# One of three shifted readings of a VectorE attention unit is made on GpSimd, with a new list of units

## The chip, the cores and the metric

The kernel runs on one core of a Trainium2 chip. The core has five engines that run their own instruction streams in order and meet only at semaphores: TensorE (PE in the profile) multiplies matrices into PSUM, ScalarE (ACT) evaluates functions such as the exponential, VectorE (DVE) and GpSimd (POOL) do elementwise arithmetic, SyncE (SP) issues DMAs. The metric is the device time of one execution in microseconds (us). Before the change it is 1565.71 us, the median of three runs (1563.85 to 1565.89).

## The reference

Two layers are computed on x of 2048 positions by 512 features. Each layer is an attention block and a gated mixer, both added to x:

```python
# attention: 32 query heads of width 16, one shared key and value head
scores = einsum('bhqd,bkd->bhqk', q, k) * 16 ** -0.5
p = softmax(scores, axis=-1)
x = x + einsum('bhqk,bkd->bhqd', p, v) @ wo          # on layernorm(x)
# mixer: width 896, mixed over the 2048 positions
z = gelu(layernorm(x) @ w_in); z1, z2 = z[:, :896], layernorm(z[:, 896:])
x = x + (z1 * (w_sp @ z2 + b_sp)) @ w_out
```

The attention has 32 x 2048 x 2048 exponentials in each layer, and they are what most of the time goes to.

## The kernel before

**Units.** The attention of a layer is cut into 32 groups (`GROUPS`; the index is gi). A group is four heads with all their 512 columns of queries, so that a tile of scores is 128 keys by 512 query columns. A group has 16 key tiles (kt), and the four heads of one key tile are a unit: four score tiles, their exponentials, and the product of these with the values (PV), which is summed over the key tiles in one PSUM bank, `PVB`. The softmax's sum comes out of the same product, from a column of ones beside the values.

**Two ways to make a unit.** `push_unit` gives a unit to ScalarE. Its blocks go through PSUM in slots of three or two blocks (`push_slot`); one ACTIVATE of L950 turns a slot into exponentials in `P_ring`. Slots alternate between a wide one (three banks) and a two-bank one; in the groups whose bit is set in `NARROW` the wide one has two blocks too. The PV of such a unit is four products at L969.

`push_unit_dve` gives a unit to VectorE. Scores come scaled so that adding a constant and writing the sum as a 16-bit integer gives the bit pattern of a bfloat16 that lies near the exponential. Four instructions of L1003 do this, one for each head, from PSUM into a tile of `big` of 128 x 2048. One such reading of the bits has a periodic error, so `NPH` = 3 readings are used: the first, and two that have 43 and 86 added to every 16-bit word (`PH_A`). These two are the instructions of L1012, each from 128 x 2048 int16 to 128 x 2048 int16 in SBUF. Each reading is multiplied with values that carry its own weight (`V_ph`), in four products at L1018, so a VectorE unit has three sets of PV products where a ScalarE unit has one. The tiles of `big` are a ring of 5, 6 or 8 (`phr`), and a tile can be written again when the PV products that read it are done.

`ON_DVE[layer][gi]` lists the key tiles of each group that VectorE makes: 245 of the 1024 units.

**Order.** The order on every engine is written out ahead of time by a planner, `_Graph.schedule`. Each operation has an engine, a planned duration, the operations it depends on and a priority (a lower number goes first). The planner runs the engines forward in planned time and lets each take the ready operation with the lowest number. `emit` then writes one fixed instruction stream for each engine, with a semaphore wait for each dependence. On VectorE the L1003 instructions have priority `P_R` = 0.3 and the L1012 ones `P_A` = 4.0. So where the next unit's scores are ready, its L1003 instructions stand ahead of the L1012 ones of this unit. Scores for VectorE units use PSUM banks that are free at that time, above all banks 5 and 7 (`side`).

**What else the engines do.** During a layer's attention, work of the same and the next layer is spread between the units: layer norms (L817, L818, L823, with `rstd` on GpSimd at L805 and L807), the projections (PE, L713), the first parts of the mixer (`b_front`, `mix_stage`; VectorE L1213, L1239, L1350), and what ends a group. At the end of a group VectorE copies the PV bank into `oT` (L1091), a DMA turns it into `ot`, and GpSimd raises the sums to the power -1 (L1048) and multiplies by them (L1061). In the last part of each layer GpSimd also takes some of the products of L1419. Where PE would have nothing to do the planner adds products with zeros or ones (L740, L751) that keep its clock up.

Of the kernel before, what the change touches and what calls it, by code (L numbers as in the profile page):

```python
# [6 lines left out]
FP32 = mybir.dt.float32  # L7
BF16 = mybir.dt.bfloat16
I16 = mybir.dt.int16
ACTF = mybir.ActivationFunctionType  # L10
ALU = mybir.AluOpType
AX = mybir.AxisListType
# [16 lines left out]
PH_A = (0, 43, 86)  # L29
# [15 lines left out]
HOLDS = 1.0  # L45

ON_DVE = ((
          (6,10,14), (6,10,14), (6,10,14), (6,10,14), (2,6,9,12,14), (2,3,12,13,14), (2,4,6,11,13),
          (3,4,6,7,9,14), (2,3,6,11), (5,7,8,13), (2,7,8,10,14), (4,5,6,12), (2,9,12,13,14), (2,9,10,13,14),
          (3,5,8), (2,6,7,14), (5,7,9,12,14), (6,8,9,10), (3,9,12,13,14), (2,7,9,13), (2,5,10,13), (2,8,11,12),  # L50
          (7,9,12,13,14), (2,7,9,12), (5,6,8,13), (4,10), (3,7,14), (2,7,10,14), (3,8,9,14), (2,9,14),
          (6,10,14), (2,9,12)
), (
          (6,10,14), (6,10,14), (10,14), (14,), (6,10,14), (6,10,14), (6,10,14), (2,10,14), (2,7,8,11),
          (6,8,10,12,14), (3,6,9,12), (3,5,8,9), (2,7,11,12,14), (2,3,9,11), (4,6,9,12), (2,4,11,12),
          (5,6,9,13), (4,6,8,9,14), (2,5,10,12), (2,7,8,10,14), (2,4,7,14), (4,8,10,11), (3,4,6,10,14),
          (6,9,12,14), (2,6,14), (2,3,12,13,14), (6,), (2,4,6,12,14), (6,8,13), (2,9,12), (3,10,11,13),
          (3,8,12)
))


# [18 lines left out]
BEFORE = ({0: 0}, {0: 0})  # L80
PRE = 6
CHAIN_ACT = 1
NARROW = (4194528, 10506244)
KEEP = 6
POOL_ON = 1
POOL_XN = 0
POOL_Z2 = 0
KEY_PR = {0: 1.2, 2: 1.7, 4: 2.2, 6: 2.4, 8: 2.7, 10: 2.9, 12: 3.2}
# [11 lines left out]
P_A = 4.0  # L100
# [64 lines left out]
class _Graph:  # L165
# [29 lines left out]
    def op(self, eng, fn, dur, r=(), w=(), prio=5, lat=0.0, chan=None, mode=0):  # L195
        task = next((x for x in (*w, *r) if isinstance(x, _Task)), None)
        o = _Op(eng, fn, dur, lat, prio, len(self.ops), chan, task, mode)
        o.chain = self.chain
        if task is not None:
            task.ops.append(o)  # L200
        if chan is not None:
            n = self.chans.setdefault(chan, 0) + 1
            self.chans[chan] = n
            o.chan_val = 16 * n

        def dep(p, kind):
            if p is o:
                return
            if p.eng == eng and p.chan is None:
                k = 0 if eng == "pe" else 1  # L210
            else:
                k = 1
            o.deps[p] = max(o.deps.get(p, 0), k)

        for key in r:
            p = self.last_w.get(key)
            if p is not None:
                dep(p, "raw")
        for key in w:
            p = self.last_w.get(key)  # L220
            if p is not None:
                dep(p, "waw")
            for q in self.readers.get(key, ()):
                dep(q, "war")
        for key in r:
            self.readers.setdefault(key, []).append(o)
        for key in w:
            self.last_w[key] = o
            self.readers[key] = []
        self.ops.append(o)  # L230
        return o
# [336 lines left out]
def bass_interleave_layers__grouped_kv_mqa__mixer_gmlp__prompt_kernel(  # L568
# [15 lines left out]
    P = 128  # L584
    NT = S // P
    QC = 512
    NQC = S // QC
    CT = QC // P
    G = _Graph(nc, (5, 7), ((0, 1, 2), (3, 4), (0, 1)))
    op = G.op  # L590
# [5 lines left out]
    def bank32(b, n=1):  # L596
        return ps32[:, 512 * b:512 * (b + n)]
# [13 lines left out]
    idle = G.sb([P, 1], FP32, "idle")  # L611
    mhalf = G.sb([P, 1], FP32, "mhalf")
    mone = G.sb([P, CT], FP32, "mone")
    X = G.sb([P, NT, D], BF16, "X")

    kT_rep = G.sb([P, 2, S], BF16, "kT_rep")
# [36 lines left out]
    NRING = 6  # L653
    big = G.sb([P, 8, 2048], BF16, "big")
    ph16 = big[:].bitcast(I16)
    wspL = big[:, 4:6, :].rearrange("p a (t q) -> p a t q", q=QC)
    gbuf32 = big[:].bitcast(FP32).rearrange("p a (b q) -> p (a b) q", q=QC)
    oT = G.sb([P, 2, QC], BF16, "oT")
# [16 lines left out]
    def BIG(r):  # L675
        return [("big", r, 0), ("big", r, 1)]
# [12 lines left out]
    def dve(fn, us, r, w, prio=5):  # L689
        return op("dve", fn, max(us - DVE_LAT, 0.06), r=r, w=w, prio=prio, lat=DVE_LAT)  # L690
# [36 lines left out]
                                         pattern=[[-1, P]], channel_multiplier=1), 0.3, r=["ident"], w=["ident"])  # L727
    op("pool", lambda e: e.memset(mhalf[:], -0.5), 0.1, w=["mhalf"])
    op("pool", lambda e: e.memset(mone[:], -1.0), 0.1, w=["mone"])
    op("pool", lambda e: e.memset(zeros[:], 0.0), 0.2, w=["zeros"])  # L730
    G.warm_after = op("pool", lambda e: e.memset(ones[:], 1.0), 0.2, w=["ones"])
    G.pvb = PVB
# [79 lines left out]
    def ln_tiles(t0, n, xT, keys, per_tile, prio=5):  # L812
# [7 lines left out]
        for t in ts:  # L820
            i = t % CT
            on_pool = POOL_XN and not G.chain and (now["layer"] or t0 >= CT or xT is xo)
            op("pool" if on_pool else "dve", lambda e, i=i, t=t: e.tensor_scalar(  # L823
# [52 lines left out]
    def q_slot(si, pr=3):  # L876
# [13 lines left out]
        if G.chain and si < CHAIN_ACT:  # L890
            op("act", lambda e: e.activation(qT[:, si % NQ, :], bank32(tk.bank), ACTF.Copy, scale=Q_SCALE), 0.48, r=[tk],
               w=[("q", si % NQ)], prio=1, lat=ACT_LAT)
# [10 lines left out]
    def next_slot():  # L903

        if main["i"] % 2:
            return 1, 3, 2
        return (2, 0, 2) if NARROW[now["layer"]] >> now["gi"] & 1 else (0, 0, 3)

# [19 lines left out]
    def push_slot(n):  # L928
# [20 lines left out]
        def act_e(e):  # L949
            return e.activation(P_ring[:, s0:s0 + n, :], bank32(b0, n).rearrange("p (k q) -> p k q", k=n), ACTF.Exp,  # L950
                                scale=E_SCALE)
# [35 lines left out]
    def push_unit_dve(u):  # L987

        hg, kt, first, last = u[:4]
        assert not first and not last  # L990
        tiles = [phr["base"] + (phr["n"] + a) % phr["ring"] for a in range(NPH)]
        phr["n"] += NPH
        first_op = None
        heads = {"left": [0, 1, 2, 3], "of": {}, "hold": HOLD_DVE[now["group"] // 8]}
        for j in range(4):
            tk = _Task()
            box = []
            o = op("pe", lambda e, box=box, tk=tk: scores(e, bank32(tk.bank), u, heads["of"][box[0]]), TILED, r=[("K", hg[1], kt), ("q", hg[0])],
                   w=[tk], prio=P_S, lat=PE_LAT, mode=1)
            o.work = WORK_OP / 4  # L1000
            o.heads = heads
            box.append(o)
            o = dve(lambda e, box=box, tk=tk: e.tensor_scalar(  # L1003
                ph16[:, tiles[0], heads["of"][box[0]] * QC:(heads["of"][box[0]] + 1) * QC], bank32(tk.bank), PH_BIAS, 0.0, op0=ALU.add, op1=ALU.max),
                0.69, [tk], BIG(tiles[0]) if j == 0 else [("phj", tiles[0], j)], P_R)
            if j == 0:
                first_op = o
            else:
                o.deps.update({q: k for q, k in first_op.deps.items() if q.task is not first_op.task})
        base = BIG(tiles[0]) + [("phj", tiles[0], j) for j in range(1, 4)]  # L1010
        for a in range(1, NPH):
            dve(lambda e, a=a: e.tensor_scalar(ph16[:, tiles[a], :], ph16[:, tiles[0], :], float(PH_A[a]), None,  # L1012
                                               op0=ALU.add), 0.69, base, BIG(tiles[a]), P_A)
        for a in range(NPH):
            def pe_pv(e, a=a):
                ins = None
                for j in range(4):
                    ins = e.matmul(bank32(PVB)[32 * j:32 * j + 32, :], V_ph[:, a, kt, :],  # L1018
                                   big[:, tiles[a], j * QC:(j + 1) * QC], tile_position=(0, 32 * j), start=False,
                                   stop=False)  # L1020
                return ins
            pv_op(pe_pv, (base if a == 0 else BIG(tiles[a])) + [("V", kt)], False, False, TILED)
# [3 lines left out]
    def finish_group(gi):  # L1026
# [15 lines left out]
        def src():  # L1042
            if not isinstance(tk, _Task):
                return ot[:, par, :, :].rearrange("p b (j r) -> p b j r", j=4)
            return bank16(tk.bank)[:, 0:CT * P].rearrange("p (b j r) -> p b j r", b=CT, j=4)
        on_pool = POOL_ON and not G.chain
        if on_pool:
# [142 lines left out]
    def b_front(t0, n, g0):  # L1190
# [8 lines left out]
        for t in ts:  # L1199
            i = t % CT  # L1200
            for h in range(2):
# [6 lines left out]
                if fine:  # L1208
                    op("act", lambda e, t=t, h=h, tk=tk: e.activation(
                        z2n[:, t, h * 448:(h + 1) * 448], bank32(tk.bank)[:, 0:448], ACTF.Gelu_apprx_tanh), 0.55,  # L1210
                        r=[tk], w=[("z2", t, h)], prio=1)
# [6 lines left out]
        for f0 in range(0, NF1, nf):  # L1218
# [16 lines left out]
            if fine:  # L1235
                op("act", lambda e, dst=dst, src=src: e.activation(dst(), src(), ACTF.Gelu_apprx_tanh), 0.60,
                   r=[tk], w=zk, prio=2)
# [6 lines left out]
        if not fine:  # L1244
            z2k = [x for t in ts for x in Z2(t)]

            def act_g(e):
                v = z2n[:, g0:t1, :]
                return e.activation(v, v, ACTF.Gelu_apprx_tanh)  # L1249
            if g0 >= Z2_LATE[now["layer"]]:  # L1250
# [11 lines left out]
    def gelu_rest():  # L1262
# [6 lines left out]
        for g0, t1 in parts:  # L1269
            k = [x for t in range(g0, t1) for x in Z2(t)]  # L1270
            v = z2n[:, g0:t1, :]
            op("act", lambda e, v=v: e.activation(v, v, ACTF.Gelu_apprx_tanh), us + 0.2 + 0.75 * (t1 - g0), r=k + ["lastexp"],
               w=k, prio=0.2)
# [204 lines left out]
    now = {"tail": False}  # L1478
# [60 lines left out]
```

## Time and profile before

| | |
|---|---|
| median of three runs | 1565.71 us (1563.85 to 1565.89) |
| the profiled execution, its own time | 1566.62 us |
| its span in the profile | 1564.7 us |
| granted TensorE clock | 0.997 |
| PE / ACT / DVE / POOL busy | 1492.9 / 1484.2 / 1379.3 / 330.3 us |
| L1003, VectorE, from PSUM | 980 of 684 ns |
| L1012, VectorE, SBUF to SBUF | 490 of 687 ns |
| L950, ScalarE, 128 x 1536 and 128 x 1024 | 538 and 751 |

The span runs from the first instruction to the last; the execution's own time has 1.9 us around it. Busy times are unions of the records of an engine, and records of successive instructions can overlap a little, as one starts while the one before it drains. A line of the profile such as "L1012 DVE TENSOR_SCALAR big<-big 128x2048 int16<-128x2048 int16 x490" names the source line, the engine, the operation, what it writes and reads with shapes and types, and how often it ran. What stands behind an arrow with an engine's name is what ended the idle time ahead of these instructions.

### The profile page before, as it was taken

The page shows a single profiled execution, that of the slowest core. Times are in us where ns is not written, and L with a number is a line of the kernel's source. Part 1 is how long each engine was busy: PE and PEld are TensorE (multiplying, and loading weights), DVE is VectorE, ACT ScalarE, POOL GpSimd, SP SyncE. Part 2 cuts the span into 40 slices and gives each one's busy share as a digit, 9 for nine tenths or more (in the row PEclk, how much of TensorE's full clock was granted, in tenths as well). Part 3 has the DMA queues.
Part 4 walks back from the last instruction along what each step waited for, and adds up shares of the span by engine and source line. Part 5 has one row for each costly group of instructions (what it writes and reads, how often), then busy time and mean ns, then how long its engine had stood idle before and what let it go on. Part 6 is the DMA issues. An engine that isn't in the chain of part 4 may idle for free.

```text
span 1564.7 us, 40919 instructions
## 1 busy us (share of the span) xinstructions
PE 1492.9 (95%) x18024; PEld 487.1 (31%) x18054; DVE 1379.3 (88%) x2368; ACT 1484.2 (95%) x1336; POOL 330.3 (21%) x319
## 2 busy tenths in 40 slices
PE   8999999999999999999999999999999999999999
PEld 3222222233333233333422222323223322323343
DVE  7989999999999888886778899999899998888887
ACT  6999999999999999999799999999999999999970
POOL 2031121212221112111210025212122211212232
PEclk9999999999999999999999999999999999999999
DMA  4501010101212433545431031110121023155472
GB/s 103 136 15 15 8 26 9 22 16 39 52 35 42 98 77 116 149 109 151 114 88 21 8 78 29 21 15 15 38 59 29 22 71 90 42 153 150 109 202 68
DMA packets 186833, 103.21 MB, mean 66 GB/s; under 512 B 151072, under 2 KB 159904, under 8 KB 186656
## 3 DMA queue, kind: packets, MB, share of 16 engines
q1 hardware_dynamic: 186656, 100.60, 25.8%
q8 instruction: 141, 2.31, 0.6%
q14 instruction: 36, 0.29, 0.1%
HBM read 34.77 MB, written 29.88 MB: 41 GB/s over the span
## 4 chain that ended last, share of the span: by engine, by line
ACT 69%; PE 24%; DVE 5%; issue 1%; DMA 1%; POOL 0%; SPq 0%; DVEq 0%
ACT P_ring L950 67%; PE ps_all L713 8%; PE ps_all L925 7%; PE ps_all L969 3%; PE ps_all L718 3%; PE ps_all L1018 3%; ACT z2n L1249 1%; DVE big L1414 1%; DVE big L1003 1%; DVE X L1114 0%; DVE st L1293 0%; DVE st L817 0%; ACT L950 0%; ACT L1249 0%; DMA X<-in_A_x_dram 0%
## 5 line engine op out<-in xcount | busy, mean ns | idle before, releaser
L950 ACT ACTIVATE P_ring<-ps_all 128x1024 bf16<-128x1024 f32 (+1 forms) x1289 | 1416.7, 1313 | 18.6 <-PE ps_all L925 17.8
L1003 DVE TENSOR_SCALAR big<-ps_all 128x512 int16<-128x512 f32 x980 | 645.0, 684 | 88.9 <-PE ps_all L925 82.8
L925 PE MATMUL ps_all<-qT,kT_rep 32*128 32x512 bf16 x4096 | 602.5, 385 | 50.2 <-ACT P_ring L950 37.2
L1048 POOL TENSOR_TENSOR rden<-ot,mone 128x16 f32<-128x16 bf16 x62 | 188.0, 3033 | 776.2 <-DMA ot<-oT 775.9
L925 PEld LDWEIGHTS ps_all<-qT,kT_rep 32*128 32x128 bf16 x4096 | 154.0, 91 | 569.4 <-ACT P_ring L950 468.3
L1012 DVE TENSOR_SCALAR big<-big 128x2048 int16<-128x2048 int16 x490 | 326.5, 687 | 3.5 <-PE ps_all L1018 0.7
L969 PE MATMUL ps_all<-P_ring,V_aug 128*32 128x512 bf16 x3116 | 296.1, 387 | 3.5 <-DVE oT L1091 2.6
L1018 PE MATMUL ps_all<-big,V_ph 128*32 128x512 bf16 x2940 | 258.7, 384 | 1.2 <-DVE big L1003 0.4
L969 PEld LDWEIGHTS ps_all<-P_ring,V_aug 128*32 128x32 bf16 x3116 | 75.8, 94 | 150.8 <-issue 122.2
L1018 PEld LDWEIGHTS ps_all<-big,V_ph 128*32 128x32 bf16 x2940 | 68.5, 94 | 97.9 <-issue 59.1
L805 POOL TENSOR_SCALAR ve<-mv 128x1 f32<-128x1 f32 (+2 forms) x44 | 16.1, 365 | 377.8 <-DVE mv L818 258.7
L713 PE MATMUL ps_all<-xnTA,z2n 128*32 128x512 bf16 x1344 | 94.8, 381 | 0.0
L713 PE MATMUL ps_all<-w_in_r,xo 128*32 128x448 bf16 x960 | 62.0, 354 | 0.2 <-DVE big L1003 0.2
L1114 DVE TENSOR_TENSOR X<-ps_all,X 128x512 bf16<-128x512 f32 x64 | 43.6, 683 | 19.1 <-PE ps_all L718 15.7
L713 PE MATMUL ps_all<-xo,w_in_r 128*32 128x256 bf16 (+1 forms) x1120 | 56.5, 317 | 0.1
L718 PE MATMUL ps_all<-w_out_r,z1c 128*128 128x512 bf16 x211 | 53.5, 381 | 2.1 <-issue 0.8
L1061 POOL TENSOR_TENSOR o_norm<-ot,rden 128x128 bf16<-128x128 bf16 (+1 forms) x118 | 53.3, 471 | 4.7
L751 PE MATMUL ps_all<-ones,zeros 128*32 128x512 bf16 x632 | 54.3, 385 | 0.0
L1350 DVE TENSOR_TENSOR big<-ps_all,big 128x512 f32<-128x512 f32 x56 | 38.2, 683 | 16.5 <-PE ps_all L713 16.1
L713 PE MATMUL ps_all<-z2n 128*32 128x512 bf16 x672 | 50.0, 382 | 0.0
L713 PE MATMUL ps_all<-z1c,z2n 128*32 128x512 bf16 x672 | 49.2, 382 | 0.0
L1419 POOL TENSOR_TENSOR z1c<-big,z1c 128x512 bf16<-128x512 f32 (+1 forms) x32 | 35.0, 1104 | 63.4 <-DVE big L1414 63.3
(99 smaller groups left out, 950.0 us busy)
## 6 DMA issues: line engine op xcount, KB each, us to landing
gp_scratch<-big SPq DMA_DIRECT2D x106, 256.0 KB, 2.1
big<-gp_scratch SPq DMA_DIRECT2D x99, 256.0 KB, 3.2
out_dram<-X SPq DMA_DIRECT2D x16, 128.0 KB, 1.7
w_in_r<-in_B_w_in_dram SPq DMA_DIRECT2D x1, 1792.0 KB, 7.9
big<-gp_scratch SPq DMA_DIRECT2D x14, 128.0 KB, 2.5
X<-in_A_x_dram SPq DMA_DIRECT2D x3, 512.0 KB, 6.5
bsp<-in_B_b_sp_dram SPq DMA_DIRECT2D x8, 128.0 KB, 3.7
ot<-oT SPq DMA_TRANSPOSE x62, 2.4
```

The source lines that it names most:

```text
L713: ins = e.matmul(out_[32 * j:32 * j + 32, :], lhs[:, 32 * j:32 * j + 32], rhs, tile_position=(0, 32 * j), start=start, stop=stop)
L718: return e.matmul(out_, lhs, rhs, start=start, stop=stop)
L751: ins = e.matmul(bank32(PVB)[32 * j:32 * j + 32, :], zeros[:, 0:32], mv, tile_position=(0, 32 * j), start=False, stop=False)
L925: return e.matmul(out, kT_rep[32 * j:32 * j + 32, a, u[1] * P:(u[1] + 1) * P], qT[32 * j:32 * j + 32, q, :], tile_position=(32 * j, 0), st ...
L950: return e.activation(P_ring[:, s0:s0 + n, :], bank32(b0, n).rearrange("p (k q) -> p k q", k=n), ACTF.Exp, scale=E_SCALE)
L969: ins = e.matmul(bank32(PVB)[32 * j:32 * j + 32, :], V_aug[:, kt, :], P_ring[:, s, :], tile_position=(0, 32 * j), start=first, stop=last)
L1003: o = dve(lambda e, box=box, tk=tk: e.tensor_scalar(ph16[:, tiles[0], heads["of"][box[0]] * QC:(heads["of"][box[0]] + 1) * QC], bank32(tk. ...
L1012: dve(lambda e, a=a: e.tensor_scalar(ph16[:, tiles[a], :], ph16[:, tiles[0], :], float(PH_A[a]), None, op0=ALU.add), 0.69, base, BIG(tiles ...
L1018: ins = e.matmul(bank32(PVB)[32 * j:32 * j + 32, :], V_ph[:, a, kt, :], big[:, tiles[a], j * QC:(j + 1) * QC], tile_position=(0, 32 * j), ...
L1048: op("pool", lambda e: e.tensor_tensor(rden[:], src()[:, :, :, DH], mone[:, :, None].to_broadcast([P, CT, 4]), ALU.pow), 3.0, r=[tk, "mone ...
L1061: op("pool", lambda e, b0=b0, nb=nb, dst=dst: e.tensor_tensor(dst, src()[:, b0:b0 + nb, :, 0:DH], rden[:, b0:b0 + nb, :, None].to_broadcas ...
L1114: dve(lambda e: e.tensor_tensor(X[:, t, :], bank32(tk.bank), X[:, t, :], ALU.add), 0.69, [tk, ("X", t)], [("X", t)], prio)
```

## The change

For 127 of the VectorE units the third reading (the one with 86 added) is made by GpSimd. The tile is looked at as 1024 words of 32 bits, and one TENSOR_TENSOR adds the word `step2`, which holds 86 in both halves (86 x 65537), read with a step of zero. No half overflows into the other, so the result has the same bits. `ON_POOL` lists these units. In the plan the addition has a duration of 2.45 us and the priority of the instruction that it replaces. One small memset at the start fills `step2`.

The list `ON_DVE` is new in almost all groups from the fifth on. It has 252 units in place of 245 (131 and 121 in the two layers, before 128 and 117), and `NARROW` marks other groups. With the slots counted from these lists, ScalarE gets 551 ACTIVATEs of three blocks (before 538), 717 of two (before 751) and one of one block.

```diff
+I32 = mybir.dt.int32
 ON_DVE = ((
-          (6,10,14), (6,10,14), (6,10,14), (6,10,14), (2,6,9,12,14), (2,3,12,13,14), (2,4,6,11,13),
+          (6,10,14), (6,10,14), (6,10,14), (6,10,14), (3,4,6,9,11,13), (2,6,7,8,11), (3,7,9,12,13),
...
-NARROW = (4194528, 10506244)
+NARROW = (8929408, 4196356)
+PADD_US = 2.45
+ON_POOL = ((
+          (6,10), (10,), (6,), (10,), (6,9), (2,7,11), (7,9,12,13), (4,6,8,10,11,14), (14,), (7,), (2,6,10,11),
...
+    step2 = G.sb([P, 1], I32, "step2")
+    ph32 = big[:].bitcast(I32)
+    op("pool", lambda e: e.memset(step2[:], PH_A[2] * 65537), 0.1, w=["step2"])
...
+        on_pool = ON_POOL[now["layer"]] and kt in ON_POOL[now["layer"]][now["gi"]]
...
         for a in range(1, NPH):
+            if a == 2 and on_pool:
+                op("pool", lambda e, a=a: e.tensor_tensor(ph32[:, tiles[a], :], ph32[:, tiles[0], :],
+                                                          step2[:, 0:1].to_broadcast([P, QC * 2]), ALU.add),
+                   PADD_US, r=base + ["step2"], w=BIG(tiles[a]), prio=P_A)
+                continue
             dve(lambda e, a=a: e.tensor_scalar(ph16[:, tiles[a], :], ph16[:, tiles[0], :], float(PH_A[a]), None,
                                                op0=ALU.add), 0.69, base, BIG(tiles[a]), P_A)
```

## The prediction, made before the changed kernel had run

> **What bounds the kernel now.** I read the page first: busy shares, then the chain that ended last, then the groups.
>
> ```profile
> span 1564.7 us, 40919 instructions
> PE 1492.9 (95%) x18024; PEld 487.1 (31%) x18054; DVE 1379.3 (88%) x2368; ACT 1484.2 (95%) x1336; POOL 330.3 (21%) x319
> ACT 69%; PE 24%; DVE 5%; issue 1%; DMA 1%; POOL 0%; SPq 0%; DVEq 0%
> L950 ACT ACTIVATE P_ring<-ps_all 128x1024 bf16<-128x1024 f32 (+1 forms) x1289 | 1416.7, 1313 | 18.6 <-PE ps_all L925 17.8
> L1003 DVE TENSOR_SCALAR big<-ps_all 128x512 int16<-128x512 f32 x980 | 645.0, 684 | 88.9 <-PE ps_all L925 82.8
> L1012 DVE TENSOR_SCALAR big<-big 128x2048 int16<-128x2048 int16 x490 | 326.5, 687 | 3.5 <-PE ps_all L1018 0.7
> ```
>
> ScalarE's exponentials are 69% of the chain, and L950 stood idle for 18.6 us in all. Two of its waits, 11.9 us at the start and 9.7 us ahead of L891 at the layers' border, belong to no attention stage. So a stage gets faster only by less ScalarE work, and slower by whatever makes L950 wait. Next, the stretches:
>
> ```profile
> 100.00:250.00 150.00, 143.13 (x1711) 42.74 (x1715) 144.11 (x242) 150.00 (x146) 41.05 (x32) 1.00 0.10 17
> 250.00:400.00 150.00, 142.12 (x1842) 45.18 (x1834) 141.61 (x244) 149.94 (x130) 34.08 (x29) 1.00 0.12 27
> 550.00:700.00 150.00, 146.38 (x2066) 48.31 (x2066) 126.92 (x218) 148.54 (x129) 28.00 (x24) 1.00 0.42 111
> 1100.00:1250.00 150.00, 145.09 (x1808) 44.10 (x1805) 140.21 (x239) 149.75 (x138) 31.27 (x26) 1.00 0.15 38
> ```
>
> The columns after the length are PE, weight loads, DVE, ACT and POOL. ACT is full everywhere. DVE is 96% busy at 100 to 250 and 85% at 550 to 700: it is the second bound early in each layer, PE later. GpSimd has room. How tightly PE hangs on VectorE is in the waits: PE's weight loads for scores (L925) waited for L1003 127 times, 40.9 us in all. The end of the scores of a slot, paired in order with its ACTIVATE, came a median 0.28 us ahead of it: that is ScalarE's cushion.
>
> **The change, ScalarE.** Three-block slots go from 538 to 551, those of two from 751 to 717 and one of one block. Start to start in unbroken runs they take a mean 1.345 and 0.92 us. So 13 x 1.345 - 34 x 0.92 + 0.5 = **-13.3 us**, all on the chain in attention. The tail after 1490 us keeps its length.
>
> **VectorE, instructions.** Seven more units: 28 more L1003. L1012 goes from 490 to 252 x 2 - 127 = 377. The records overlap, and successive ones start 0.60 us apart:
>
> ```profile
> 164.33 0.68 DVE L1012 TENSOR_SCALAR big<-big 128x2048 int16<-128x2048 int16 x1
> 164.93 1.28 DVE L1003 TENSOR_SCALAR big<-ps_all 128x512 int16<-128x512 f32 x2
> 166.13 0.68 DVE L1012 TENSOR_SCALAR big<-big 128x2048 int16<-128x2048 int16 x1
> ```
>
> (28 - 113) x 0.60 = -51 us of VectorE's work. That is off the chain, beside ACT, worth 0 by itself; it is what lets ScalarE shed seven units.
>
> **GpSimd, the addition.** No row has it. The nearest are products of two inputs, undisturbed: 128x256 in 0.67 us and 128x512 in 1.157 us (L1419), so 0.19 us plus 1.9 ns an element; 1024 words give 2.13 us. From L1061 (0.40 and 0.62 us at 128 and 256) the same line gives 1.93. The upper end is the plan's own 2.45. I take 2.13, the row nearest in size: 127 x 2.13 = 270 us, POOL 600 us, 39% of the span. Its queue is in order: behind an addition that waits for its readings stand L1048 (2.9 us), L1061 and `rstd`, and behind those the DMAs that turn the output and PE's projections. These have the span of a group as cover (POOL waited 775.9 us for `ot`), so 0; without cover each would be up to 2.1 us late. The memset of `step2` (0.10 us, as L729) lies under the first load: 0.
>
> **What VectorE pays.** This decides the case:
>
> ```profile
> 804.39 1.16 POOL L1419 TENSOR_TENSOR z1c<-big,z1c 128x512 bf16<-128x512 f32 x1
> 804.46 1.56 DVE L823 TENSOR_SCALAR xn<-X,mv,rs 128x512 bf16<-128x512 bf16 x2 [0.81 <-POOL rs L807]
> 1008.57 0.76 POOL L1061 TENSOR_TENSOR o_norm<-ot,rden 128x128 bf16<-128x128 bf16 x2
> 1008.97 1.51 DVE L1012 TENSOR_SCALAR big<-big 128x2048 int16<-128x2048 int16 x2
> 1249.24 1.47 DVE L1012 TENSOR_SCALAR big<-big 128x2048 int16<-128x2048 int16 x2
> 1249.24 1.73 POOL L1061 TENSOR_TENSOR o_norm<-ot,rden 128x128 bf16<-128x128 bf16 x2
> 216.91 0.66 DVE L1012 TENSOR_SCALAR big<-big 128x2048 int16<-128x2048 int16 x1
> 217.08 0.58 POOL L805 TENSOR_SCALAR ve<-mv 128x4 f32<-128x4 f32 x1 [16.04 <-DVE mv L818]
> ```
>
> A fast SBUF instruction of VectorE that starts while GpSimd streams stands still until GpSimd ends: L823, median 0.404 us, took 1.239 when it began 0.07 us after L1419; the first L1012 at 1008.97 took 0.904. An L1012 then lasts the rest of GpSimd's run plus 0.546 us, so it loses that rest less 0.14. The other way round GpSimd waits: L1061 took 0.92 in place of 0.40 at 1249.24. L1003, which reads PSUM, shows no such loss (693 ns at most).
>
> The Trainium skill, "SBUF — State Buffer", section "Who interferes with whom", states this as an exclusive lock between VectorE's two-port modes and GpSimd, held for a whole instruction by whichever issues first. The trace agrees for streaming instructions; beside the 2.9 us powers of L1048, L1012 kept its 0.69 us, so "whole" holds not for those. By the skill's words the sum below would be the same.
>
> Who is first? GpSimd starts 0.085 us after the fourth L1003 ends (as L805 after L818), VectorE's next record 0.085 us before it ends. An L1012 that stands right behind wins; one behind another L1003 loses. Put an addition of 2.13 us on every one of the 245 units of before: in 114 it blocks nothing, 66 lose over 1 us (mean 1.50), 35 lose 0.5 to 1 (mean 0.83), 30 less; 0.555 us a unit. For 127 units: 34, 18 and 16 units, together 70 us (57 at 1.93, 93 at 2.45). So **VectorE's gain of 51 us is more than spent**: +19 us against before.
>
> **From VectorE to the chain.** A late VectorE keeps a PSUM bank, PE stops in order at its next score, and the next slot's scores come late. Below, nothing arrives (all within VectorE's 185 us of idle time): 0. Above, all of it: 70, or 93. Between: the cushion takes 0.28 off each loss, leaving 34 x 1.22 + 18 x 0.55 = 51 us. Of L1003's 980 instructions some 250 had PE already waiting (sum over the groups waiting for it), 139 had VectorE waiting for PE; the rest lie between, so I take half: +25.5 us.
>
> **PE.** Seven units at L1018 add 2 x 4 products each; a tiled set of four costs about 0.2 us more pitch, so 3 us, under the fillers of L751 (54.3 us): 0, at most 3. PE now waits for GpSimd for the third reading: where VectorE won, it ends 0.085 + 0.6 + 2.1 = 2.8 us after the reading against a planned 2.45: some 0.3 us late in about 50 units, the size of the cushion: 0, at most 15.
>
> **Sum.** 1566.6 (the profiled execution) - 13.3 + 25.5 = 1578.8. That execution stands 0.9 us over the median, so I give **1578 us**.
>
> **Rivals.** *The blocks are swallowed* (faster). For it: DVE idles 185 us, the average load hardly changes (51 freed, 70 spent), and with one L1012 fewer queued the other may follow its L1003 at once and win the port; if four losses in five land in idle time, 10 us arrive. Against: 96% load at 100 to 250. It decides where under 13 of the 51 us arrive; without any, 1565.7 - 13.3 = 1552, with ten 1562. *VectorE becomes the bound.* In groups 4 to 11 of the first layer (40 units for 38, 22 with the addition) it needs 2 x 6 x 0.60 - 22 x 0.60 + 22 x 0.55 = +6 us where about 6 of 165 are idle, while ScalarE gives up 4. If this holds in all the tight stretches all 70 us less what is idle there arrive: 1597 to 1622. *The addition is not what the rows say*: integers of 32 bits could run slower. The Trainium skill, "GPSIMD Engine Reference", section "Performance versus the Vector engine", gives 4497 ns for a 2048-element fp32 addition; half of it, 2.25 us, is an estimate from that page and no run here shows it. At 2.45 the middle sum gives 1566.6 - 13.3 + 25.5 x 93 / 70 - 0.9 = 1586. *They cancel*: within 0.2% (3.1 us), about what a measurement of this kernel can tell from no change.
>
> **Chances.** The forecast, with its dearer addition, 1569 to 1597: 0.42. Swallowed, 1551 to 1562: 0.37. VectorE bound, 1597 to 1622: 0.14. Cancel: 0.07. So faster 0.37, same 0.07, slower 0.56. The range 1553 to 1606 leaves out the best cases of one side and most of the VectorE bound; the forecast's own range is 1569 to 1597.
>
> **What would show it.** The addition near 2.1 us, in blocked cases 2.7; L950 with 551 and 718 runs; L1012 x377 with a mean of about 0.87 us (70 us over 377) and L1003 unchanged; L950's idle time for L925 up from 18 to some 43 us; longer waits of PE's L925 for L1003 and L1012. I am wrong if L1012 keeps 0.69 us (no collisions), or is slow while L950 still does not wait (swallowed), or if DVE turns up with a large share of the chain.

## The result, and the profile after

The changed kernel takes 1605.36 us (median of four runs, 1600.04 to 1609.83) against 1565.36 us for the kernel before, now also of four runs: 1.0256 times as long, 95% interval 1.0223 to 1.0288. The prediction had 1578 us with 1553 to 1606 as its range: the sign was right, the size (12 us more) was a third of what came (40 us more). The profiled execution is the fastest of the four, 1600.04 us, and has a span of 1598.2 us.

The page of the changed kernel: busy shares, the chain, and the groups that the change touches (L964 is the old L950, L1018 the old L1003, L1032 the old L1012, L1028 the addition).

```profile
span 1598.2 us, 40759 instructions
PE 1496.1 (94%) x17943; PEld 489.4 (31%) x17973; DVE 1387.9 (87%) x2283; ACT 1481.0 (93%) x1316; POOL 601.6 (38%) x447
ACT 47%; PE 30%; DVE 20%; issue 2%; DMA 1%; POOL 1%; SPq 0%; DVEq 0%
L964 ACT ACTIVATE P_ring<-ps_all 128x1536 bf16<-128x1536 f32 (+1 forms) x1269 | 1413.4, 1276 | 56.3 <-PE ps_all L939 53.6
L1018 DVE TENSOR_SCALAR big<-ps_all 128x512 int16<-128x512 f32 x1008 | 663.0, 684 | 100.9 <-PE ps_all L939 94.8
L1028 POOL TENSOR_TENSOR big<-big,step 128x1024 int32<-128x1024 int32 x127 | 271.4, 2137 | 417.0 <-DVE big L1018 401.5
L1032 DVE TENSOR_SCALAR big<-big 128x2048 int16<-128x2048 int16 x377 | 306.1, 828 | 4.7 <-PE ps_all L1038 1.2
```

L1032 runs 113 times less, but each takes a mean 828 ns in place of 687. VectorE as a whole is busy for 1387.9 us, 8.6 us more than before, with seven units more. Its share of the chain goes from 5% to 20%, and L964 waits for its scores for 53.6 us, before 17.8. The stretches from 100 to 400 us and from 1100 to 1250 us show where:

```profile
100.00:250.00 150.00, 135.59 (x1582) 39.98 (x1574) 142.24 (x216) 140.80 (x127) 78.48 (x49) 0.97 0.09 16
250.00:400.00 150.00, 139.63 (x1773) 43.20 (x1770) 138.20 (x224) 145.20 (x129) 64.36 (x44) 1.00 0.11 29
1100.00:1250.00 150.00, 140.78 (x1852) 47.05 (x1855) 138.82 (x225) 146.54 (x127) 72.70 (x47) 1.00 0.14 33
```

The columns behind the length are PE, weight loads, DVE, ACT and POOL. ACT was full here and now lacks 3 to 9 us in each of them. One collision, from 1021 us on, by selected lines in order of time (the bracket is idle time of the engine and what ended it):

```profile
1021.17 1.89 POOL L1028 TENSOR_TENSOR big<-big,step 128x1024 int32<-128x1024 int32 x1 [3.60 <-DVE big L1018]
1021.54 2.07 DVE L1032 TENSOR_SCALAR big<-big 128x2048 int16<-128x2048 int16 x1
1022.01 0.39 PE L939 MATMUL ps_all<-qT,kT_rep 32*128 32x512 bf16 x3
1023.53 1.27 DVE L1018 TENSOR_SCALAR big<-ps_all 128x512 int16<-128x512 f32 x2
1023.67 0.40 PE L1038 MATMUL ps_all<-big,V_ph 128*32 128x512 bf16 x4 [1.26 <-DVE big L1032]
1024.27 0.62 PE L726 MATMUL ps_all<-xnTA,wq_r 128*32 128x256 bf16 x16 [0.20 <-DVE big L1018]
1025.26 1.45 ACT L964 ACTIVATE P_ring<-ps_all 128x1536 bf16<-128x1536 f32 x1 [1.46 <-PE ps_all L939]
```

GpSimd starts its addition at 1021.17 while VectorE is busy with an L1233. VectorE's second reading starts at 1021.54, stands still until GpSimd ends at 1023.06, and takes 2.07 us in place of 0.69. PE, whose next products in order are those of that reading, sits idle for 1.26 us, and for another 0.20 us at the product behind them, which waits for a late first reading. ScalarE then sits idle for 1.46 us. The loss of 1.38 us arrives whole.

### The profile page after: what moved, and what is told of

Read it like the earlier page. It is cut to its first block, busy times and chain, and to the rows that moved or that the text cites. A ratio compares the mean times of both kernels' runs of the same rounds, so it can differ in the third digit from the quotient of the medians.

```text
span 1598.2 us, 40759 instructions
## 1 busy us (share of the span) xinstructions
PE 1496.1 (94%) x17943; PEld 489.4 (31%) x17973; DVE 1387.9 (87%) x2283; ACT 1481.0 (93%) x1316; POOL 601.6 (38%) x447
## 3 DMA queue, kind: packets, MB, share of 16 engines
q1 hardware_dynamic: 186656, 100.60, 25.1%
## 4 chain that ended last, share of the span: by engine, by line
ACT 47%; PE 30%; DVE 20%; issue 2%; DMA 1%; POOL 1%; SPq 0%; DVEq 0%
ACT P_ring L964 45%; PE ps_all L939 10%; DVE big L1018 8%; PE ps_all L726 8%; DVE big L1032 6%; PE ps_all L983 4%; PE ps_all L1038 4%; PE ps_all L731 3%; ACT z2n L1269 1%; DVE X L1134 1%; DVE st L831 1%; DVE xn L837 1%; DVE big L1434 1%; DVE oT L1111 1%; DVE z2n L1233 0%
## 5 line engine op out<-in xcount | busy, mean ns | idle before, releaser
L964 ACT ACTIVATE P_ring<-ps_all 128x1536 bf16<-128x1536 f32 (+1 forms) x1269 | 1413.4, 1276 | 56.3 <-PE ps_all L939 53.6
L1018 DVE TENSOR_SCALAR big<-ps_all 128x512 int16<-128x512 f32 x1008 | 663.0, 684 | 100.9 <-PE ps_all L939 94.8
L939 PE MATMUL ps_all<-qT,kT_rep 32*128 32x512 bf16 x4096 | 605.6, 387 | 59.4 <-ACT P_ring L964 34.7
L1028 POOL TENSOR_TENSOR big<-big,step 128x1024 int32<-128x1024 int32 x127 | 271.4, 2137 | 417.0 <-DVE big L1018 401.5
L939 PEld LDWEIGHTS ps_all<-qT,kT_rep 32*128 32x128 bf16 x4096 | 154.8, 91 | 578.2 <-ACT P_ring L964 403.3
L1032 DVE TENSOR_SCALAR big<-big 128x2048 int16<-128x2048 int16 x377 | 306.1, 828 | 4.7 <-PE ps_all L1038 1.2
L983 PE MATMUL ps_all<-P_ring,V_aug 128*32 128x512 bf16 x3088 | 292.9, 389 | 2.0 <-DVE oT L1111 1.2
L1038 PE MATMUL ps_all<-big,V_ph 128*32 128x512 bf16 x3024 | 268.9, 387 | 17.0 <-DVE big L1032 16.1
L1038 PEld LDWEIGHTS ps_all<-big,V_ph 128*32 128x32 bf16 x3024 | 70.9, 94 | 126.8 <-issue 65.2
L726 PE MATMUL ps_all<-xnTA,z2n 128*32 128x512 bf16 x1344 | 94.6, 381 | 0.9 <-DVE big L1018 0.9
L1134 DVE TENSOR_TENSOR X<-ps_all,X 128x512 bf16<-128x512 f32 x64 | 43.7, 685 | 23.3 <-PE ps_all L731 18.8
L726 PE MATMUL ps_all<-w_in_r,xo 128*32 128x448 bf16 x960 | 60.2, 354 | 1.5 <-DVE big L1018 1.3
L726 PE MATMUL ps_all<-xo,w_in_r 128*32 128x256 bf16 (+1 forms) x1120 | 56.7, 317 | 0.5 <-DVE big L1018 0.3
L731 PE MATMUL ps_all<-w_out_r,z1c 128*128 128x512 bf16 x212 | 53.3, 381 | 2.2 <-issue 0.8
L726 PE MATMUL ps_all<-z1c,z2n 128*32 128x512 bf16 x672 | 48.5, 382 | 0.9 <-DVE big L1018 0.9
L726 PE MATMUL ps_all<-z2n 128*32 128x512 bf16 x672 | 48.7, 382 | 0.1
```

Of the source, the lines that this page charges most:

```text
L726: ins = e.matmul(out_[32 * j:32 * j + 32, :], lhs[:, 32 * j:32 * j + 32], rhs, tile_position=(0, 32 * j), start=start, stop=stop)
L731: return e.matmul(out_, lhs, rhs, start=start, stop=stop)
L939: return e.matmul(out, kT_rep[32 * j:32 * j + 32, a, u[1] * P:(u[1] + 1) * P], qT[32 * j:32 * j + 32, q, :], tile_position=(32 * j, 0), st ...
L983: ins = e.matmul(bank32(PVB)[32 * j:32 * j + 32, :], V_aug[:, kt, :], P_ring[:, s, :], tile_position=(0, 32 * j), start=first, stop=last)
L1018: o = dve(lambda e, box=box, tk=tk: e.tensor_scalar(ph16[:, tiles[0], heads["of"][box[0]] * QC:(heads["of"][box[0]] + 1) * QC], bank32(tk. ...
L1028: op("pool", lambda e, a=a: e.tensor_tensor(ph32[:, tiles[a], :], ph32[:, tiles[0], :], step2[:, 0:1].to_broadcast([P, QC * 2]), ALU.add), ...
```

## The experiments

Theory A says that these collisions make ScalarE late almost in full. Its rivals were B, that the new places and the planner's order are dearer by themselves, C, that PE waits for GpSimd's result, later D, that GpSimd's cut additions come late, and E and F on the way that the loss takes.

**The new lists with everything on VectorE.**

```diff
-        on_pool = ON_POOL[now["layer"]] and kt in ON_POOL[now["layer"]][now["gi"]]
+        on_pool = False
```

> New lists of units (252) and the new NARROW, all three readings on VectorE, nothing on GpSimd. Theory A (collisions: a fast SBUF instruction of VectorE that stands still for a GpSimd addition makes ScalarE late almost in full): no collisions are left and ScalarE keeps its 13 us less, VectorE's load goes up by 7 units x 6 x 0.60 = 25 us to about 1404 us; 1552 to 1566 us. Rival B (the new places and the order that the planner makes of them are dearer by themselves): near the changed kernel, 1595 to 1605. Rival C (PE waits for GpSimd's reading, which comes later than planned): as A.

Measured: 1628.43 us, 1.0398 times the kernel before (1.0376 to 1.0420). All three missed. Nothing collides here:

```profile
L964 ACT ACTIVATE P_ring<-ps_all 128x1024 bf16<-128x1024 f32 (+1 forms) x1269 | 1410.7, 1295 | 85.4 <-PE ps_all L939 83.7
L1032 DVE TENSOR_SCALAR big<-big 128x2048 int16<-128x2048 int16 x504 | 335.3, 689 | 6.3 <-PE ps_all L1038 3.6
```

and yet ScalarE waits for 83.7 us, more than with the collisions. VectorE has 24 us more to do here than in the kernel before (1403.3 us busy against 1379.3), but it still idles for 14% of the span. With the addition on GpSimd the planner writes another order from the same list; whether the list or the order is at fault this run can't tell.

**The addition with the lists of before.** `ON_DVE` and `NARROW` as before, the addition in every second unit:

```diff
+        on_pool = phr["unit"] % 2 == 0        # phr["unit"] counts VectorE's units
```

> The lists and NARROW of before (245 units), with the addition on GpSimd in every second unit (122). A: 122 x 0.42 us (53.1 us over 127 in the changed kernel's trace) = 51 us of losses, most of them arriving, and no shorter ScalarE work: 1600 to 1615. B: the places are the old ones, so 1560 to 1570. C: 1590 to 1615, with L1032 at its 0.69 us.

Measured: 1666.96 us (1.0641, 1.0619 to 1.0663), 52 us above the range that A gave. L1033, the second and third readings here, takes a mean 880 ns: 66 of 368 lose, together 71 us. The collisions are there, and something more.

**No streaming on GpSimd.** In its place a power of 10 numbers, which lasts about as long:

```diff
-op("pool", lambda e, a=a: e.tensor_tensor(ph32[:, tiles[a], :], ph32[:, tiles[0], :], step2..., ALU.add),
+op("pool", lambda e, a=a: e.tensor_tensor(phf32[:, tiles[a], 0:10], powin[:], mone..., ALU.pow),
```

> The changed kernel in its own order, but GpSimd does not make the third reading: in the same place, with the same waits and after about the same time (an estimate of 1.97 us from 1.04 us for 4 and 2.90 us for 16 elements), it raises 10 numbers to the power -1 and writes them into the tile. So the third reading of 127 units is left out of the computation. In the trace of before L1048, the same operation, did not hold up L1012. A: L1032 back at 0.69 us and the time at 1550 to 1560. B: 1595 to 1605, as lists and order are the changed kernel's. C: 1595 to 1605, as PE waits for GpSimd as before.

Measured: 1568.15 us (1.0020, 1.0009 to 1.0030), 8 us above A's range. The fill of the ring that this kernel needs at its start holds GpSimd up, and the first ACTIVATE of L968 begins at 27.0 us, in the changed kernel at 13.6. Without it:

> As the run without the addition, but without the fill of the ring that delayed its start by 13 us: the first two additions are made, and in the other 125 units GpSimd raises 10 numbers to the power -1 in place of the third reading, which is left out. Theory A (the collisions are the whole loss, and the 13 us less of ScalarE's work are there once they are gone): 1568.2 - 13.1 = 1555, between 1552 and 1558. Rival C (waiting for GpSimd's late result costs something too): over 1560.

Measured: **1555.69 us, 0.9939 times the kernel before (0.9926 to 0.9953)**. With the same lists, the same order and a GpSimd that is busy for as long, the 49.7 us are gone, and the 10 us under the kernel before are most of the 13.3 that ScalarE's shorter work was to bring:

```profile
L969 ACT ACTIVATE P_ring<-ps_all 128x1536 bf16<-128x1536 f32 (+1 forms) x1269 | 1404.8, 1314 | 23.0 <-PE ps_all L944 22.1
L1038 POOL TENSOR_TENSOR big<-phw,mone 128x10 f32<-128x10 f32 x125 | 274.5, 2197 | 368.2 <-DVE big L1023 352.8 <-DVE mv L837 14.0 <-DVE big L1042 1.2
L1042 DVE TENSOR_SCALAR big<-big 128x2048 int16<-128x2048 int16 x377 | 255.9, 695 | 4.7 <-PE ps_all L1048 1.2
```

GpSimd needs 2.20 us for each here, as long as the addition, so waiting for its result (C) costs nothing to speak of. Nor is VectorE held up: 54 readings start while such a power runs, and they take 685 ns in the mean, 695 at most. In the changed kernel 50 start under an addition and take 1723 ns in the mean. It is the streaming that costs, where GpSimd reads and writes whole tiles. B cannot hold for the changed kernel's own lists in their own order.

**The addition in parts.** The same words in two, four or eight instructions; the planner is told the same 2.45 us, so that every engine's order stays:

```diff
-e.tensor_tensor(ph32[:, tiles[a], :], ph32[:, tiles[0], :], step2[:, 0:1].to_broadcast([P, QC * 2]), ALU.add)
+w = QC * 2 // 4
+for h in range(4):
+    ins = e.tensor_tensor(ph32[:, tiles[a], h * w:(h + 1) * w], ph32[:, tiles[0], h * w:(h + 1) * w],
+                          step2[:, 0:1].to_broadcast([P, w]), ALU.add)
```

> The changed kernel with the addition cut into two instructions of 512 words, some 1.0 us each, so that VectorE can have its turn between the two. A: no L1032 stands still for over about 1.0 us, L1032's mean goes from 0.83 us to about 0.75, half of the losses are gone: 1572 to 1588. B and C: 1597 to 1607 (GpSimd takes a little longer for the two halves).

> The changed kernel with the addition cut into four instructions of 256 words. From 1.89 us for 1024 and 1.00 us for 512 words an instruction of 256 lasts an estimated 0.55 us, 2.2 us for four, still under the planned 2.45. A: an L1032 stands still for at most some 0.4 us, about what ScalarE's cushion (0.28 us) and VectorE's idle time take up: L1032's mean 0.72 to 0.74 us, 1555 to 1563 us, faster than the kernel before. Rival D (GpSimd, now the one that waits for VectorE three times in an addition, hands over its reading late, and PE waits for it): 1568 or more.

> Eight instructions of 128 words, an estimated 0.33 us each, 2.7 us in all, over the planned 2.45. A: still less standing still for L1032, 1554 to 1563. D: the third reading comes 0.3 us or more late, PE waits for GpSimd, later than with four parts: 1565 or more.

Measured: halves 1570.23 us (1.0038, 1.0025 to 1.0051), **quarters 1559.46 us (0.9966, 0.9952 to 0.9979)**, eighths 1599.62 us (1.0217, 1.0203 to 1.0231). The halves come out 2 us below A's range, the quarters inside it, the eighths as D had it. Four parts beat the changed kernel by 46 us and the kernel before by 6. The groups of the kernel with four parts:

```profile
L964 ACT ACTIVATE P_ring<-ps_all 128x1536 bf16<-128x1536 f32 (+1 forms) x1269 | 1406.5, 1301 | 22.5 <-PE ps_all L939 20.7
L1031 POOL TENSOR_TENSOR big<-big,step 128x256 int32<-128x256 int32 x508 | 345.7, 710 | 345.5 <-DVE big L1018 324.1
L1036 DVE TENSOR_SCALAR big<-big 128x2048 int16<-128x2048 int16 x377 | 266.7, 723 | 4.7 <-PE ps_all L1042 1.2
```

L1036 is back near 0.69 us, and ScalarE's wait for scores at 20.7. A part lasts 0.61 us undisturbed, and no reading loses more than 0.44 us. With eight parts L1036 does about as well in the mean (741 ns), and 65 of its 68 blocked readings lose at most 0.32 us. But three did not get in between two parts: they stood still over several and took 4.70, 4.44 and 2.65 us. Why those three, no run shows. Above all an addition lasts a mean 3.33 us from the start of its first part to the end of its last, and D comes true. The waits of that kernel:

```profile
PEld ps_all L1042 <- POOL big L1031: 47.8, 61, 2.7
PE ps_all L1042 <- POOL big L1031: 27.9, 38, 2.2
```

The columns are us in total, times, the longest. PEld, the weight loads, and PE, the products behind them, wait in part at the same time, so the two lines must not be added. The weight loads wait 47.8 us for GpSimd, with four parts, where an addition takes 2.72 us, 11.4 us in 32 waits. The order was written for 2.45.

**Half of the collisions, each as long as before.** Whole additions in every second of the 127 units, powers in the others:

> The changed kernel in its own order, with whole additions in every second of the 127 units (64), and 10 powers in place of the third reading, which is left out, in the other 63. Half of the collisions, each as long as before: L1042's losses some 26 us of 53. If each collision reaches ScalarE by itself, half of the 50 us between 1555.7 and 1605.4 comes back: 1576 to 1586. If the losses add up from one to the next and only the sum of many finds no idle time (or the lower TensorE clock of the changed kernel makes it worse the more there are): clearly less than half of them arrive, 1560 to 1572.

Measured: 1580.83 us (1.0095, 1.0077 to 1.0113). What arrives is 1580.83 - 1555.69 = 25.1 us, half of 49.7, as if each collision counted by itself. Beside the halves this run is the sharpest comparison, because the sums of the losses are alike:

| run | blocked readings | losing over 1 us | lost | arrives (over 1555.69) | arrives, profiled executions (over 1558.25) |
|---|---|---|---|---|---|
| changed kernel | 53 | 30 | 52.9 us | 49.7 us | 41.8 us |
| every second unit | 30 | 18 | 29.8 us | 25.1 us | 26.7 us |
| halves | 64 | 0 | 30.5 us | 14.5 us | 11.6 us |
| quarters | 61 | 0 | 13.6 us | 3.8 us | 1.2 us |

Counted are the second and third readings over 715 ns, each less 689 ns, in the profiled execution. The fifth column compares medians, the last one the executions in which the losses were counted. Thirty microseconds lost in long pieces cost 25 us, the same in pieces of under 0.9 us cost 14.5. If of each reading only what it loses beyond 0.28 us counts, the cushion of the prediction, 39.2, 22.2, 14.9 and 2.2 us are left. The layer norms' SBUF instructions (L837, L1321 and the same lines of the other kernels) lose 6.9, 4.6, 3.9 and 2.5 us more than in the run with powers. Together that is 46.1, 26.8, 18.8 and 4.7 us, against 49.7, 25.1, 14.5 and 3.8 measured: the sums are right to within 5 us, with the long pieces arriving a little more than so reckoned and the short ones a little less.

**Was VectorE the bound?** The measured time lies in the range that the prediction gave to this rival, so it needs an answer. VectorE is busy for 1365.4 us with every second unit and for 1362.2 with the halves, and the losses are alike, yet the times are 10.6 us apart; a sum of work would make them alike. The changed kernel and the run with powers also have the same 1304 ACTIVATEs in the same order, so ScalarE's lateness can be read at each of them. Over the work that the run with powers does from 900 to 1400 us, ScalarE falls 23.5 us behind. The readings lose 25.4 us there (19.6 beyond 0.28 each), and VectorE has 47.9 us of idle time there in the run with powers. So the losses arrive where VectorE has time to spare, and not only in the tight stretches early in a layer.

**The way of the loss.** In PE's order alone, the products of the second reading are put up to 1.5 us later:

```diff
+        for o in self.late:       # the products of the second reading of the 127 units
+            o.t0 = max(o.t0, min([o.t0 + LATE_US] + [x.t0 - 0.01 for x, _ in o.succ]))
+        order["pe"].sort(key=lambda o: o.t0)
```

> The changed kernel, whole additions and collisions as they are, every engine but PE in the same order. In PE's order the PV products of the second reading (L1046, the ones that wait for an L1032 that stands still) of the 127 units stand up to 1.5 us of planned time later, with nothing else moved. Theory E (the losses reach ScalarE because these products, in order ahead of the next slot's scores, wait for the reading): PE's waits for L1032 fall from 52 us to under 20 and the time to 1565 to 1585, while L1032 keeps losing some 50 us. Theory F (the losses arrive through PSUM banks that a late VectorE frees late, the prediction's path): 1598 to 1612, plus up to 6 us for some 58 more changes between kinds of products.

> The same move by up to 1.0 us in the kernel with four parts. It shows what the move itself costs where hardly anything collides, and whether it wins more: E: 1555 to 1562; if more changes between kinds of products cost PE time on the path: 1562 to 1570.

Measured: 1626.89 us with whole additions (1.0386, 1.0360 to 1.0411), 1567.28 us with four parts (1.0014, 1.0004 to 1.0024). With whole additions both ranges are missed, E's by 42 us and F's by 9. With four parts the move by up to 1.0 us costs 7.8 us (1567.28 against 1559.46); what a move by up to 1.5 us costs without collisions was not run. PE's waits for VectorE, first in the kernel before, then in the changed kernel, then with the products moved (L1037 is the second reading there, L1023 the first, and L944, L731 and L1043 are the old L939, L726 and L1038):

```profile
PEld ps_all L925 <- DVE big L1003: 40.9, 127, 0.7
PEld ps_all L1018 <- DVE big L1012: 12.8, 46, 0.5
```

```profile
PEld ps_all L939 <- DVE big L1018: 61.3, 164, 1.4
PEld ps_all L1038 <- DVE big L1032: 35.7, 65, 1.8
PEld ps_all L726 <- DVE big L1018: 18.1, 54, 1.6
PE ps_all L1038 <- DVE big L1032: 16.1, 22, 1.5
PE ps_all L939 <- DVE big L1018: 15.3, 39, 1.1
```

```profile
PEld ps_all L944 <- DVE big L1023: 74.7, 175, 1.6
PEld ps_all L731 <- DVE big L1023: 24.9, 54, 2.0
PE ps_all L944 <- DVE big L1023: 22.3, 46, 1.3
PEld ps_all L1043 <- DVE big L1037: 11.3, 33, 1.0
```

The weight loads' waits for the second reading fall from 35.7 to 11.3 us, as E had it, while L1037 still loses 51.7 us. Those for the first readings, which free the PSUM banks, rise in their place: from 61.3 to 74.7 us and from 18.1 to 24.9. E falls, as the time did not come down with its waits: whichever of VectorE's results PE needs next comes late, and if it isn't this one it is the bank. F alone is not the way either, since in the changed kernel PE waits for both. The waits don't show which part of the 21.5 us over the changed kernel is the move's own price.

**Order and list.** The lists of before with the addition in four parts, and the four-part kernel with nothing but the planner's number for the addition changed (`PADD_US` 2.45 to 2.75):

> The lists of before with the addition in every second unit, as in the second run, cut into four. If collisions are what took that run to 1667 us (L1033 lost 0.19 us x 368 = 70 us there): 1600 or less, as 65 or so come back. If collisions were the whole of its loss: 1565 to 1572. What stays above that is the order that the planner makes when it puts the old places beside the new durations.

> The kernel with four parts, same lists and the same instructions; only the planner is told 2.75 us in place of 2.45 for the addition, nearer to the 2.72 us that its four parts take in the trace. Rival B, in its new form (a list of units fits only the order that it was made for, and any other order is dearer by tens of us, with or without collisions): 1590 to 1625. If only work and collisions count: 1555 to 1562, PE's waits for GpSimd gone.

Measured: 1613.09 us (1.0299, 1.0269 to 1.0328), above both of its ranges, and 1617.88 us (1.0331, 1.0315 to 1.0346). The first gets back 53.9 of the 101 us by which the second run had been slower, and the collisions account for most of that: beyond 0.28 us each the readings lost 53.8 us in the second run and lose 4.1 here. The rest, 47 us, is there with hardly a collision that counts. The other is the clean case: same lists, same instructions, same collisions (the readings' mean is 728 ns, 723 in the kernel with four parts, and the losses beyond 0.28 us are 2.5 us and 2.2), and another number in the planner costs 58.4 us. ScalarE's wait for scores is 65.5 us there against 20.7:

```profile
L964 ACT ACTIVATE P_ring<-ps_all 128x1536 bf16<-128x1536 f32 (+1 forms) x1269 | 1409.0, 1290 | 67.2 <-PE ps_all L939 65.5
L1036 DVE TENSOR_SCALAR big<-big 128x2048 int16<-128x2048 int16 x377 | 268.2, 728 | 5.5 <-PE ps_all L1042 2.3
```

So an order alone can cost some 50 us. That fits what the first two runs have too much, but their share of order was not measured apart. In three kernels a planner with other durations made a dearer order from one of the two lists; how the lists were chosen is not on record, and why one order is so much better than another was not followed further.

## Why the prediction was wrong, point by point

- **ScalarE's 13.3 us less: right in the main.** With 551 and 717 slots and hardly a collision the time is 1555.69 us, 10 us under the kernel before; the "swallowed" rival's 1552 us is 4 us off. Where the other 3 us went is open.
- **The addition's price: a little dear.** Forecast 2.13 us with 1.93 as the lower end. Undisturbed it lasts 1.89 us, behind a reading that came first 2.40. That the mean is 2.14 is chance, as the waiting for VectorE is in it. The rows of L1061 were the better guide than the row nearest in size. The Trainium skill's figure ("GPSIMD Engine Reference", section "Performance versus the Vector engine") had given an estimate of 2.25 us: too dear for this addition.
- **Who blocks whom: right.** L1018 keeps 684 ns. Forecast: 34 units that lose over 1 us and 70 us in all, 57 with the shorter addition; measured 30 and 52.9 us. The layer norms, which lose 6.9 us more, were not in the count. What the Trainium skill states in "SBUF — State Buffer", section "Who interferes with whom", the runs bear out for streaming: whichever starts first goes on, and the other stands still. The powers of 2.2 us that hold nobody up are the exception that the prediction had read in the trace of before.
- **The arrival at ScalarE: the step that failed.** The working had 51 us left after the cushion and took half of it, "the rest lie between, so I take half: +25.5 us". No row gave that half. Measured, the readings' losses beyond the cushion are 39.2 us, with the layer norms 46.1, and 49.7 us arrive (41.8 in the profiled executions): all of it and not half. The way was also told too narrowly. The prediction had PE stop only at a PSUM bank that VectorE frees late; the weight loads' waits for the first readings do rise, from 40.9 to 61.3 us at the scores, but those for the second reading, at its products, rise from 12.8 to 35.7. Idle time of VectorE that lies between its instructions does not absorb a late one here, because PE's order is fixed and its next wait is for VectorE, whether for the second reading or for a bank. VectorE is idle for 12% of the span before and 13% after, and it does not help.
- **Where the number owes something to luck:** without the halving the sum would have been 1566.6 - 13.3 + 51 - 0.9 = 1603.4 us, 2 us from the measured time. But the 51 rested on 70 us of losses where 52.9 came, and it left out the layer norms; two errors cancel there. The sign came right on a chance of 0.56, and the time lies 0.6 us inside the stated range, in the part that the prediction gave to VectorE as the bound. Its own sign of being wrong came true: VectorE's share of the chain went from 5% to 20%.
- **GpSimd's late result: right to leave out** at the plan's 2.45 us, as the run with the powers shows. Eight parts show what it costs when it is late by 0.9 us: 47.8 us of waits of PE's weight loads, in a kernel that is 40 us slower than with four parts; the three readings that stood still for long, 9.7 us of losses together, have a share in it too.
- **What VectorE was to gain, and what the places cost:** of the 51 us less of instructions 42.4 are seen (1336.9 us busy in the run with the powers against 1379.3), and the collisions take them back. The prediction took it for granted that the new places are as good as the old ones. In the changed kernel's own order they are; with another order the same list costs some 50 us more.

## What to carry to other kernels

Before moving an elementwise instruction from VectorE to GpSimd, count which of VectorE's fast SBUF instructions will start while GpSimd streams, and how long the longest stands still: where orders are fixed and PE waits for VectorE next, as here, the loss beyond the bound engine's cushion arrives nearly whole, however much idle time VectorE's average shows. If the work has to be there, cut it into parts so short that what one blocked instruction loses is about that cushion, but not so many that the result misses its planned time: here four parts turned 2.6% slower into 0.3% faster, and eight gave nearly all of it back (2.2% slower). Where a planner writes the order, one of its numbers can be worth more than the change that is being measured: hold the order fixed when the cause of a difference is sought.

## What the runs showed of the hardware that was not expected

In the changed kernel the granted TensorE clock is low in places where PE has been held up. One of them, behind a reading of 2.38 us at 938.2:

```profile
940.00:945.00 5.00, 4.14 (x34) 0.77 (x30) 3.69 (x7) 3.97 (x4) 0.07 (x1) 0.59 0.13 26
945.00:950.00 5.00, 5.00 (x66) 1.62 (x62) 4.94 (x7) 3.91 (x5) 4.91 (x2) 0.72 0.15 30
```

The clock (third column from the end) is 0.59 and 0.72 in these ten microseconds, and ScalarE is busy for 7.88 of them. Over the span it is 0.988, in the kernel before 0.997, and with four parts 0.997. Being slow is not enough for it: the run with everything on VectorE and the one planned with 2.75 us are slower still, at 0.994 and 0.996. The four executions of the changed kernel go along with the clock, from 1600.0 us at 0.988 to 1609.8 at 0.982, so it may be a part of why 49.7 us arrive by the medians and 41.8 in the profiled executions. It isn't shown: no run holds the clock up with the collisions in place, and in the ten microseconds above ScalarE falls 2.7 us behind the run with powers, no more than the 3.0 us that the two readings at 938.2 and 945.5 us lose.

An instruction of few elements on GpSimd, even of 2.2 us, does not hold VectorE up (readings that start under one take 685 ns in the mean), while 1.89 us of streaming does. What counts seems to be how long GpSimd reads and writes, not how long its record lasts; the trace shows the records alone.
